# Copying the split state into an order by part before it goes to the output product's stack

## The chip, the core and the metric

The kernel runs on one core of a Trainium2 chip. Its engines are named as the profile names them: PE (matrix products; PEld is its weight load), DVE, ACT and POOL (elementwise work) and SP, which here only issues DMA transfers; ACT issues some transfers as well. An engine works through its own list of instructions in order and waits on semaphores for the others. The metric is the device time of one execution in microseconds (us). Before the change the median of three runs is 1157.68 us (1153.25 to 1157.78).

## The reference

A recurrence runs over 768 steps for 4 batches of 8 heads, each with a state of 40 x 40; its outputs, laid out as 3072 tokens of 320 numbers, pass through two gated layers.

```python
for t in range(S):
    kt, vt, rt = (k[:, :, t], v[:, :, t], r[:, :, t])
    wt, at, bt = (w[:, :, t], a[:, :, t], b[:, :, t])
    y[:, :, t] = np.einsum('bhd,bhde->bhe', rt, state)
    Sa = np.einsum('bhde,bhe->bhd', state, at)
    state_decay = state * wt[:, :, None, :] - np.einsum('bhd,bhe->bhde', Sa, bt)
    state = state_decay + np.einsum('bhd,bhe->bhde', vt, kt)

h = x @ w_in                     # 320 -> 2048
g = where(h >= 1, h, where(h <= -1, 0, (h + 1) ** 2 / 4))
x = g @ w_out                    # 2048 -> 320
g = x @ w_gate                   # 320 -> 1536
out = (g / (1 + exp(-g)) * (x @ w_val)) @ w_out2
```

## The kernel before, in words

The 768 steps are cut into 12 chunks of 64, and each chunk into four tasks, one for each batch (8 heads, 320 columns of state). Three streams of work share the engines.

- **Preparation** (`decay_tasks`, `p_tasks`, `inv_tasks`): products of the decays, the scaled inputs, the 64 x 64 matrices of a chunk, and on DVE the inverse of its triangular part, 31 steps of two small instructions (lines 915 and 920). The inverse is stored to `tsd` (line 938) and comes back for a task pair as `tt` (lines 1009 and 1013).
- **State** (`m_tasks`): a task multiplies the inputs with the state (line 1038), takes two rounds through the halves of the inverse (lines 1048 and 1054, with ACT and DVE splits at 1062, 1073 and 541 between them), forms the output product and the new state on PE (lines 1106 and 1127), and scales the state on DVE (1134, 1137).
- **Layers** (`in1`, `in2`, `outp`): 12 blocks of 256 tokens through both layers, PE lines 1170 and 1234, as each chunk's outputs come ready. Their weights arrive in pieces (line 607) that DVE (612 to 620), ACT and POOL bring into 16-bit form.

All numbers that PE multiplies are 16-bit pairs, a high and a low part. The new state is split so into the tile `ss`, partitions 64 to 103: for each head 120 columns, the parts high, low and high of 40 columns each (line 1140 on ACT, the helper `split`, line 541, on DVE). From `ss` it goes two ways. A transposing DMA (line 1148) makes `s0t[j]`, which the next chunk's line 1038 reads. And three DMAs (line 1152) put the three parts under each other into the stack `s0s[j]`, partitions 0 to 119, which the output product (line 1127) of the next chunk reads. Since a part of one head is 40 numbers wide, each of the three moves 40 partitions x 8 heads in runs of 80 bytes, 320 runs:

```python
for i in range(3):
    DMA(lambda e, i=i: e.dma_start(
        out=s0s[j][D * i:D * i + D], in_=G("ss", key)[q, :, D * i:D * i + D]),
        r=[("ss", n)], w=[("s0s", n)], use=SS, p=p + 8, dma=0.25, cost=0.84)
```

There are 44 tasks with such a state (none in the last chunk), so 132 of these DMAs and 42,240 runs.

The order of all instructions is planned when the kernel is built (class `Plan`). Each piece of work is recorded as a task with its engine, an assumed cost, what it reads and makes, the buffers it uses, and a due time `p`. The plan runs the tasks in a model of the engines, forwards and backwards in turn, and keeps the best order; a DMA goes to SP's list, or to ACT's where SP is busy in the model. A buffer of a pool (`ss` has one tile, and a second one for the first four tasks) is held from its first use to the end of its last, a DMA's landing included. Line 1265 holds the constants that set the due times: `LEAD` is how far ahead of its place in the period the state work of a chunk is due, `PLEAD` how far ahead of that the preparation, `BP` and `BM` shift chunk 0's, `DP` parts the halves of the decay work, `LSTEP` spaces the later weights. The tile `gf` is 128 partitions high, and only partitions 64 to 127 are written.

Of the kernel before, what the change touches and what calls it, by code (L numbers as in the profile page):

```python
# [8 lines left out]
F32 = mybir.dt.float32  # L9
F16 = mybir.dt.float16  # L10
# [312 lines left out]
def tile_recurrence__then__gated_mlps(  # L323
# [16 lines left out]
    B, H, S, D = r.shape  # L340
    BH = B * H
    HD = H * D
    C = 64
# [27 lines left out]
    v_, s_, p_, t_ = nc.vector, nc.scalar, nc.gpsimd, nc.tensor  # L371

    K = Plan()
    T, G = K.task, K.get

    def sbt(name, shape, dt, n=None):
        if n is None:
            return sb.tile(shape, dt, name=name)
        ts = [sb.tile(shape, dt, name=f"{name}{i}") for i in range(n)]
        K.pool(name, ts)  # L380
        return ts
# [25 lines left out]
    ss = sbt("ss", [128, H, 128], F16, 1)  # L407
    s0t = [sbt(f"s0t{i}", [128, H, 48], F16) for i in range(B)]
    s0s = [sbt(f"s0s{i}", [128, H, D], F16) for i in range(B)]
# [4 lines left out]
    sbt("vh", [128, H, D], F16, 1)  # L414
    sbt("xs", [128, H, D], F16, 2)
    sbt("tt", [128, 2, 2, H, HC], F16, 1)
    sbt("gf", [128, H, C], F32, 1)
    sbt("pf", [128, H, C], F32, 1)
    mx = sbt("mx", [128, 36 * NT], F16)
    K.pool("xt", [mx[:, 6 * NT * i:6 * NT * (i + 1)].rearrange("p (a t) -> p a t", a=6)  # L420
# [552 lines left out]
    def m_tasks(n, p):  # L973
        c, j = divmod(n, B)
# [4 lines left out]
        key, pk, mp = ("m", n), ("p", n), ("mp", n // 2)  # L979
        q = slice(64, 64 + D)  # L980
        VH, VS, PX, VT, WT, SS = (
            [(x, key)] for x in ("vh", "vss", "px", "vsT", "wt", "ss"))
# [7 lines left out]
        for o in (0, C):  # L990
            DMA(lambda e, o=o: e.dma_start(
                out=G("ldv", key)[o:o + C], in_=v[j, :, cs, :].rearrange("h t e -> t h e")),
                w=[(key, "v")], use=V, p=p - 4, dma=0.53)
        T("ACT", c_s(HD), lambda: s_.activation(
            out=G("ldv", key), in_=G("ldv", key), func=AF.Copy, scale=2.0**8), r=[(key, "v")],
          w=[(key, "vd")], use=V, p=p - 2)
        if j % 2 == 0:
            ps = slice(8 * j, 8 * j + 16)
            DMA(lambda e: e.dma_start(
                out=G("wa", mp).rearrange("p j h d -> p (j h) d"),  # L1000
                in_=was[c % 4, ps].rearrange("h t e -> t h e")),
                r=[("dec", c)], w=[(mp, "wa")], use=WA, p=p + 4, dma=1.06)
            if not last:
                DMA(lambda e: e.dma_start(
                    out=G("ff", mp)[q].rearrange("p j h d -> p (j h) d"),
                    in_=fdr[c][ps].unsqueeze(0).to_broadcast([D, 2 * H, D])),
                    r=[("f", c)], w=[(mp, "f")], use=FF, p=p + 4, dma=0.36, cost=0.68)
            td = tsd[c][:, :, :, ps]
            DMA(lambda e: e.dma_start(
                out=G("tt", mp)[0:64].rearrange("p f j h t -> p f (j h t)"),  # L1010
                in_=td.rearrange("f l s b t -> (l s) f (b t)")),
                r=[("tsd", c)], w=[(mp, "tt")], use=TT, p=p - 3, dma=0.5)
            DMA(lambda e: e.dma_start(
                out=G("tt", mp)[64:96].rearrange("p f j h t -> p f (j h t)"),
                in_=td[:, 0].rearrange("f s b t -> s f (b t)")),
                r=[("tsd", c)], w=[(mp, "tt")], use=TT, p=p - 3, dma=0.25, cost=0.68)

        T("ACT", c_s(HD), lambda: s_.activation(  # L1018
            out=G("vh", key), in_=G("ldv", key), func=AF.Copy),
          r=[(key, "vd")], w=[(key, "vh")], use=V + VH, p=p - 1)  # L1020
        e0, eng, cost = side(c in VLP, HD)
# [59 lines left out]
        for hf in range(2):  # L1081
# [3 lines left out]
              use=PX + XS[hf], p=p)  # L1085
# [45 lines left out]
        if not last:  # L1131
            y = lambda: hd(G(pg, (key, "y")))[q]
            if c:
                T("DVE", c_v(HD, True), lambda: v_.tensor_tensor(
                    out=y(), in0=y(), in1=sf[j][q], op=ALU.add),
                  r=[(key, "y"), ("sf", n - B)], w=[(key, "s1")], use=PY, p=p)
            T("DVE", c_v(HD), lambda: v_.tensor_tensor(
                out=y(), in0=y(), in1=G("ff", mp)[q, j % 2], op=ALU.mult),
              r=[(key, "s1") if c else (key, "y"), (mp, "f")], w=[(key, "s2")], use=PY + FF, p=p)
            T("ACT", c_s(2 * HD), lambda: s_.activation(  # L1140
                out=hi2(G("ss", key)[q]), in_=two(y()), func=AF.Copy, scale=2.0**-6),
              r=[(key, "s2")], w=[(key, "s3")], use=PY + SS, p=p)
            T("DVE", c_v(HD), lambda: split(
                G("ss", key)[q, :, D:2 * D], y(), 2.0**-6, G("ss", key)[q, :, 0:D]),
              r=[(key, "s3")], w=[("ss", n)], use=PY + SS, p=p)
            T("ACT", c_s(HD), lambda: s_.copy(out=sf[j][q], in_=y()), r=[(key, "s2")],
              w=[("sf", n)], use=PY, p=p)
            TR(lambda: nc.sync.dma_start_transpose(
                out=s0t[j], in_=flat(G("ss", key)[64:112])),
                r=[("ss", n)], w=[("s0t", n)], use=SS, p=p, dma=0.57)  # L1150
            for i in range(3):
                DMA(lambda e, i=i: e.dma_start(
                    out=s0s[j][D * i:D * i + D], in_=G("ss", key)[q, :, D * i:D * i + D]),
                    r=[("ss", n)], w=[("s0s", n)], use=SS, p=p + 8, dma=0.25, cost=0.84)
        xk = ("x", c, j // 2)
        xf = lambda: G("pf", (key, "x"))[vr].rearrange("p h t -> p (h t)")[:, 0:HD]
        XF = [("pf", (key, "x"))]
# [104 lines left out]
                    out=out[r0:r0 + C, :], in_=o()[64 * q:64 * q + 64]),  # L1262
                    r=[(ok, tt, 1)], w=[("out", c)], use=[("u", uk)], p=p, dma=0.31)

    PER, LEAD, PLEAD, DLEAD, WLEAD, ILEAD, WSTEP, LPRI, LSTEP, BP, BI, BM, DP, BD, P1, M1 = 69.67, 10.07, 94.28, 203.97, -34.92, 128.76, 0.3, 29.05, 2.22, -0.71, 2.76, 0.74, 10.0, 113.83, 18.78, 5.0
    SUP = PER / B

    def m0(n):
# [112 lines left out]
```

## Time and profile before

| | |
|---|---|
| median of 3 runs | 1157.68 us (1153.25 to 1157.78) |
| the profiled execution, its own time | 1155.31 us |
| its span on the core | 1153.6 us |
| PE busy in the span | 910.4 us (79%) |
| ACT, DVE, POOL busy | 866.0, 755.0, 569.0 us |
| DMA packets | 560948, of which 537140 under 512 bytes |

The profile is of one execution. Busy time leaves out the issuing of DMAs, which is listed as SPq or ACTq with the time that the instruction held that engine's list. An entry "A <- B" in a list of waits is idle time of A that ended when B was done; "issue" there is time in which the engine waited for nothing that the profile shows. PEclk is the granted TensorE clock, 1.00 for 2.4 GHz and 0.50 for 1.2 GHz.

### The profile page before, as it was taken

To read this page: it belongs to the slowest core of one execution; us is meant where nothing else is said; L and a number is where in the kernel's file an instruction comes from. 1 tells how busy PE (TensorE), PEld (TensorE's weight loads), DVE (VectorE), ACT (ScalarE), POOL (GpSimd) and SP (SyncE) were. 2 spreads that over 40 slices of the span, in tenths; PEclk is the share of its full clock that TensorE was granted. 3 is DMA by queue.
4 is the path that set the end of the run, shared out by engine and by line. 5 is a ranking of instruction groups with operands and counts; after the bars stand their busy time and mean duration, and the time that the engine had idled before them with its cause. 6 is when DMAs were issued, how large, how long until landed. Compare 5 with 4: busy or idle time off the path is not lost. (4 is left out here: it accounts for less than half of the span.)

```text
span 1153.6 us, 29900 instructions
## 1 busy us (share of the span) xinstructions
PE 910.4 (79%) x11328; PEld 745.1 (65%) x11328; DVE 755.0 (65%) x1830; ACT 866.0 (75%) x1628; POOL 569.0 (49%) x756
## 2 busy tenths in 40 slices
PE   0131246744789899989999899999999999999998
PEld 0131235533567777777777787787777777888886
DVE  7778796886879487585765856856758457442211
ACT  2595687876996998988979979788798796763422
POOL 5689634533566536545554545545545433322321
PEclk9999999766899999999999999999999999999999
DMA  9988699669979888787977877799667534321000
GB/s 212 240 200 169 182 149 159 147 116 197 195 145 152 122 124 143 134 129 126 147 121 126 134 123 128 127 134 140 103 130 129 101 75 76 60 44 32 4 15 23
DMA packets 560948, 144.63 MB, mean 125 GB/s; under 512 B 537140, under 2 KB 544820, under 8 KB 560804
## 3 DMA queue, kind: packets, MB, share of 16 engines
q1 hardware_dynamic: 523036, 135.08, 64.8%
q10 hardware_dynamic: 37768, 7.66, 4.3%
q8 instruction: 88, 1.44, 0.6%
q14 instruction: 56, 0.46, 0.2%
HBM read 74.87 MB, written 18.14 MB: 81 GB/s over the span
## 5 line engine op out<-in xcount | busy, mean ns | idle before, releaser
L539 POOL TENSOR_TENSOR mx<-mx 128x512 f16<-128x512 f32 x168 | 194.7, 1161 | 271.8 <-ACT mx L1190 252.1
L1234 PE MATMUL po<-wo,mx 128*128 128x320 f16 x2016 | 314.3, 302 | 3.9 <-DVE mx L541 2.5
L1234 PEld LDWEIGHTS <-mx 128*128 128x128 f16 x2016 | 191.1, 98 | 72.9 <-DVE mx L541 2.8
L1170 PE MATMUL ph<-mx,w 128*128 128x256 f16 x1536 | 194.0, 278 | 17.4 <-DMA mx<-x 10.1
L1170 PEld LDWEIGHTS <-w 128*128 128x128 f16 x1536 | 147.6, 99 | 41.7 <-issue 18.4
L1170 PE MATMUL ph<-x2t,wv 128*128 128x256 f16 x1152 | 141.3, 272 | 4.9 <-DVE mx L1220 3.2
L1170 PE MATMUL ph<-x2t,wg 128*128 128x256 f16 x1152 | 140.9, 273 | 2.3 <-ACT mx L1216 2.2
L1190 ACT CAST mx<-mx 128x512 f16<-128x512 f32 x168 | 102.9, 615 | 48.1 <-DVE mx L1220 30.1
L1206 DVE SCALAR_TENSOR_TENSOR mx<-ph,mx 128x512 f32<-128x512 f32 x96 | 66.2, 690 | 94.6 <-ACT mx L1203 94.2
L1170 PEld LDWEIGHTS <-wv 128*128 128x128 f16 x1152 | 110.4, 98 | 20.0 <-issue 6.5
L1170 PEld LDWEIGHTS <-wg 128*128 128x128 f16 x1152 | 109.8, 98 | 17.7 <-issue 2.9
L920 DVE TENSOR_TENSOR pg<-pg,ub 128x126 f32<-128x126 f32 (+22 forms) x372 | 96.4, 259 | 9.8
L915 DVE SCALAR_TENSOR_TENSOR ub<-ub,pg 128x126 f32<-128x126 f32 (+22 forms) x372 | 92.4, 248 | 14.5 <-DMA ub<-lsd 4.5
L1220 DVE SCALAR_TENSOR_TENSOR mx<-ph,mx 128x512 f32<-128x512 f32 x72 | 49.4, 686 | 71.9 <-PE ph L1170 69.0
L1062 ACT ACTIVATE xs<-px 32x320 f16<-32x320 f32 x176 | 75.0, 426 | 11.6 <-PE px L1054 6.1
L545 POOL TENSOR_TENSOR ldp<-ldp 128x320 f32<-128x320 f32 (+1 forms) x90 | 76.6, 864 | 11.8 <-ACT ldp L822 5.5
L1073 ACT ACTIVATE vss<-px 32x640 f16<-32x640 f32 x88 | 61.1, 695 | 12.3 <-PE px L1048 10.3
L1048 PEld LDWEIGHTS <-tt 96*32 96x32 f16 x768 | 28.5, 95 | 64.4 <-issue 45.2
L541 DVE SCALAR_TENSOR_TENSOR xs<-px,xs 32x320 f16<-32x320 f32 x88 | 42.6, 484 | 39.7 <-ACT xs L1062 37.3
L1202 ACT ACTIVATE mx<-ph 128x512 f32<-128x512 f32 x96 | 57.0, 594 | 12.6 <-PE ph L1170 10.5
L539 POOL TENSOR_TENSOR vss<-ldv,vh 128x320 f16<-128x320 f32 x48 | 38.5, 801 | 56.5 <-ACT vh L1018 25.0
L541 DVE SCALAR_TENSOR_TENSOR vss<-px,vss 32x320 f16<-32x320 f32 x88 | 43.4, 493 | 30.0 <-ACT vss L1073 24.8
(226 smaller groups left out, 1713.9 us busy)
## 6 DMA issues: line engine op xcount, KB each, us to landing
ldv<-in_v_dram SPq DMA_DIRECT2D x88, 80.0 KB
ub<-lsd SPq DMA_DIRECT2D x22, 256.0 KB
wo<-in_moe_w_out_dram SPq DMA_DIRECT2D x17, 320.0 KB
ldp<-was SPq DMA_DIRECT2D x23, 160.0 KB
out_dram<-mx SPq DMA_DIRECT2D x46, 80.0 KB
wo<-in_moe_w_in_dram SPq DMA_DIRECT2D x7, 512.0 KB
ldp<-in_b_dram SPq DMA_DIRECT2D x22, 160.0 KB
ldp<-wks SPq DMA_DIRECT2D x22, 160.0 KB
```

Source lines behind the costliest of these rows:

```text
L539: e.tensor_tensor(out=out, in0=x, in1=hi, op=ALU.subtract)
L541: e.scalar_tensor_tensor(out=out, in0=x, scalar=scale, in1=hi, op0=ALU.mult, op1=ALU.subtract)
L545: e.tensor_tensor(out=out, in0=x, in1=y, op=ALU.mult)
L915: v_.scalar_tensor_tensor(out=t, in0=L()[:, j, j + 1:].unsqueeze(1).to_broadcast([128, nm, ni]), scalar=-(2.0**-10), in1=m[:, 0:nm, j:j + ...
L920: v_.tensor_tensor(out=m[:, 0:nm, j + 1:], in0=m[:, 0:nm, j + 1:], in1=t, op=ALU.add)
L1062: s_.activation(out=xs[32 * i:32 * i + 32], in_=px[32 * hf:32 * hf + 32], func=AF.Copy, scale=-(2.0**-10))
L1073: s_.activation(out=hi2(G("vss", key)[z]), in_=two(hd(G("px", key))[z]), func=AF.Copy, scale=2.0**-8)
L1170: t_.matmul(out=ps, lhsT=wts[:, wi, fs], rhs=xT[:, xi, :], start=(i == 0), stop=(i == len(plan) - 1))
L1190: T("ACT", c_s(512), lambda: s_.copy(out=G("g", key)[:, 0], in_=u2(key)), r=[(key, "u")], w=[(key, "gh")], use=U + GG, p=p)
L1202: s_.activation(out=u2(key), in_=ps2(key), func=AF.Relu, scale=2.0**-8, bias=1.0)
L1206: T("DVE", c_v(512, True), lambda: v_.scalar_tensor_tensor(out=u2(key), in0=ps2(key), scalar=2.0**8, in1=u2(key), op0=ALU.max, op1=ALU.min ...
L1234: t_.matmul(out=ps, lhsT=g[:, x, f, 128 * tt:128 * tt + 128], rhs=wo[:, 2 * i + f, y, :], start=(i == 0 and f == 0 and m == 0), stop=(i == ...
```

## The change

The three parts are first copied, by one DVE instruction, into a new place `s2` of 40 partitions x 3 parts x 320 numbers, so that the eight heads of one part lie side by side. The three DMAs then read `s2` and write whole rows of the stack: each moves 40 runs of 640 bytes. `s2` is one buffer, in partitions 0 to 39 of `gf`, which were not used; the copy of a task cannot start before the three DMAs of the task before have landed. `ss` is now released when the copy and the transposing DMA are done. The plan's assumed costs for these DMAs go down, the copy is added with an assumed cost of 0.33 us, and six of the constants are changed.

```diff
-    sbt("gf", [128, H, C], F32, 1)
+    gf = sbt("gf", [128, H, C], F32, 1)[0]
+    K.pool("s2", [gf[0:D].rearrange("p h t -> p (h t)").bitcast(F16)[:, 0:3 * HD].rearrange(
+        "p (x y) -> p x y", x=3)])
...
+            S2 = [("s2", key)]
+            T("DVE", 0.06 + 3 * HD * 0.28e-3, lk=True, emit=lambda: v_.tensor_copy(
+                out=G("s2", key).rearrange("d x (h e) -> d x h e", h=H),
+                in_=G("ss", key)[q, :, 0:3 * D].rearrange("d h (x e) -> d x h e", x=3)),
+              r=[("ss", n)], w=[(key, "s2c")], use=SS + S2, p=p + 4)
             for i in range(3):
                 DMA(lambda e, i=i: e.dma_start(
-                    out=s0s[j][D * i:D * i + D], in_=G("ss", key)[q, :, D * i:D * i + D]),
-                    r=[("ss", n)], w=[("s0s", n)], use=SS, p=p + 8, dma=0.25, cost=0.84)
+                    out=s0s[j][D * i:D * i + D].rearrange("d h e -> d (h e)"), in_=G("s2", key)[:, i]),
+                    r=[(key, "s2c")], w=[("s0s", n)], use=S2, p=p + 8, dma=0.11, cost=0.68)
...
-    ... LEAD, PLEAD, ... LSTEP, BP, ... BM, DP ... = ... 10.07, 94.28, ... 2.22, -0.71, ... 0.74, 10.0 ...
+    ... LEAD, PLEAD, ... LSTEP, BP, ... BM, DP ... = ... 16.61, 96.27, ... 2.43, -5.96, ... 2.65, 6.56 ...
```

The new costs and constants move instructions on every engine, mostly by a few places. Of the 132 DMAs into the stack 98 are now issued by SP and 34 by ACT (87 and 45 before); over all transfers SP issues 945 and ACT 78 (932 and 91 before). Line numbers of the changed kernel are larger by 2 to 7.

The first place is SP's list where chunk 0's inverse is stored (`tsd_138`) and fetched again (`tt_115`); `wo_67`, `was` and `wks` are transfers of weights and of later decays. Before:

```order
L938 DMA tsd_138<-ub_121 32x32x32 x4
L607 DMA wo_67<-in_moe_w_out_dram 128x640
L864 DMA lsd_139<-gf_116 32x8x32
L729 DMA was_159<-wg 128x640
L729 DMA wks_160<-wg 128x640
L607 DMA wo_67<-in_moe_w_in_dram 128x2x512
L1009 DMA tt_115<-tsd_138 64x2x512
L1013 DMA tt_115<-tsd_138 32x2x512
```

Now, at the same place:

```order
L940 DMA tsd_138<-ub_121 32x32x32 x4
L866 DMA lsd_139<-gf_116 32x8x32
L609 DMA wo_67<-in_moe_w_out_dram 128x640
L1011 DMA tt_115<-tsd_138 64x2x512
L609 DMA wo_67<-in_moe_w_out_dram 128x640
L1015 DMA tt_115<-tsd_138 32x2x512
L866 DMA lsd_139<-gf_116 32x8x32 x2
L609 DMA wo_67<-in_moe_w_in_dram 128x2x512
```

The pair of decay stores now stands ahead of the `tsd` store, and the weight piece of 512 KB behind the fetch; a piece of 320 KB stands between its two halves.

The second place is DVE's list at the state of the first task of chunk 1: `ss_100` is the split state, lines 915 and 920 (917 and 922) are steps of a later chunk's inverse, `xs_114` the split that PE's line 1048 waits for. Before:

```order
L541 SCALAR_TENSOR_TENSOR xs_114<-px_124,xs_114 32x320
L915 SCALAR_TENSOR_TENSOR ub_121<-ub_121,pg_126 128x100
L612 TENSOR_SCALAR px_125<-wo_67 128x512
L920 TENSOR_TENSOR pg_126<-pg_126,ub_121 128x4x25
L541 SCALAR_TENSOR_TENSOR ss_100<-pg_127,ss_100 40x8x40
L915 SCALAR_TENSOR_TENSOR ub_121<-ub_121,pg_126 128x96
```

Now:

```order
L543 SCALAR_TENSOR_TENSOR ss_100<-pg_126,ss_100 40x8x40
L917 SCALAR_TENSOR_TENSOR ub_121<-ub_121,pg_127 128x81
L1154 COPY gf_116<-ss_100 40x960
L543 SCALAR_TENSOR_TENSOR xs_114<-px_124,xs_114 32x320
L922 TENSOR_TENSOR pg_127<-pg_127,ub_121 128x3x27
L614 TENSOR_SCALAR px_125<-wo_67 128x320
```

The state's split moved ahead of the next task's `xs`, and the copy (`gf_116` is the tile that holds `s2`) stands between the two, so that `xs` starts only after the copy.

## Rows read from the trace of the kernel before

**Rows 1.** Busy time by stretch: us, us (instructions) per engine, clock, DMA share, GB/s
```profile
core 0: us, PE busy (x) PEld busy (x) DVE busy (x) ACT busy (x) POOL busy (x), PEclk, DMA share, GB/s
0.00:180.00 180.00, 41.51 (x616) 35.67 (x617) 144.76 (x399) 114.07 (x197) 124.04 (x243) 1.00 0.88 189
180.00:320.00 140.00, 85.47 (x1081) 64.80 (x1081) 110.61 (x232) 110.15 (x210) 58.87 (x69) 0.78 0.83 163
320.00:1000.00 680.00, 633.91 (x8137) 521.27 (x8134) 462.67 (x1141) 575.18 (x1100) 344.04 (x404) 1.00 0.75 124
```
**Rows 2.** PE's waits over the run: us in total, times, longest
```profile
PE px L1048 <- DVE xs L541: 24.5, 27, 2.8
...
PE ph L1048 <- DMA tt<-tsd: 11.0, 2, 7.6
...
PE px L1054 <- DVE vss L541: 9.1, 13, 1.8
...
PE pg L853 <- DMA kbT<-lsp: 1.7, 2, 1.2
```
**Rows 3.** Timeline 108 to 126 us, queues and PE: start, duration, instruction
```profile
116.12 0.40 SPq L607 DMA_DIRECT2D wo<-in_moe_w_in_dram  x1
...
117.27 0.62 SPq L1013 DMA_DIRECT2D tt<-tsd  x1
...
121.87 0.42 PE L1048 MATMUL ph<-xs,tt 96*32 96x40 f16 x8 [7.64 <-DMA tt<-tsd]
```
**Rows 4.** The chain of work that ended last: start, duration of two transfers
```profile
707.64 2.10 DMA s0s<-ss
749.58 2.16 DMA tt<-tsd
```
**Rows 5.** Issues of the state's and of a 40-row transfer: duration ns min/median/max
```profile
L1152 SPq DMA_DIRECT2D s0s<-ss x83: 767/852/1429, 158.2 to 985.4; - x83
L1152 ACTq DMA_DIRECT2D s0s<-ss x43: 783/822/872, 154.9 to 982.6; - x43
...
L1004 SPq DMA_DIRECT2D ldp<-fdr x19: 301/463/1897, 57.2 to 945.5; - x19
L1004 ACTq DMA_DIRECT2D ldp<-fdr x3: 307/309/353, 152.2 to 528.2; - x3
```
**Rows 6.** Timeline 144 to 147 us, ACT's list and engine
```profile
144.75 1.42 ACTq L1152 DMA_DIRECT2D s0s<-mx  x1
...
146.22 0.47 ACT L956 ACTIVATE x<-pf 64x320 f16<-64x320 f32 x1 [0.94 <-issue]
```
**Rows 7.** Packets of the run and the main DMA queue, and the state's transfers
```profile
DMA packets 560948, 144.63 MB, mean 125 GB/s; under 512 B 537140, under 2 KB 544820, under 8 KB 560804
...
q1 hardware_dynamic: 523036, 135.08, 64.8%
...
s0s<-ss SPq DMA_DIRECT2D x83, 25.0 KB
```
**Rows 8.** DVE instructions by line: duration ns min/median/max, shapes
```profile
L723 DVE COPY wg<-wv x11: 172/175/179, 22.4 to 124.8; 32x40 f32<-32x40 f32 x11
...
L856 DVE TENSOR_TENSOR pg<-pg,mask x48: 677/699/700, 59.3 to 945.4; 128x512 f32<-128x512 f32 x48
...
L541 DVE SCALAR_TENSOR_TENSOR wg<-lsp,wg x2: 685/944/1202, 269.5 to 315.3; 64x512 f16<-64x512 f32 x2
```
**Rows 9.** DVE's waits over the run
```profile
DVE xs L541 <- ACT xs L1062: 37.3, 42, 3.6
DVE vss L541 <- ACT vss L1073: 26.6, 30, 2.4
```
**Rows 10.** Timeline 320 to 350 us, one state and its transfers
```profile
325.87 0.49 DVE L541 SCALAR_TENSOR_TENSOR ss<-pg,ss 40x320 f16<-40x320 f32 x1
...
339.38 0.83 SPq L1152 DMA_DIRECT2D s0s<-ss  x1
...
346.74 0.49 DVE L541 SCALAR_TENSOR_TENSOR ss<-pg,ss 40x320 f16<-40x320 f32 x1 [0.77 <-ACT ss L1140]
```

More of the change, by code (lines that the diff above doesn't have):

```diff
@@ L1263, in outp @@
                     r=[(ok, tt, 1)], w=[("out", c)], use=[("u", uk)], p=p, dma=0.31)
-    PER, LEAD, PLEAD, DLEAD, WLEAD, ILEAD, WSTEP, LPRI, LSTEP, BP, BI, BM, DP, BD, P1, M1 = 69.67, 10.07, 94.28, 203.97, -34.92, 128.76, 0.3, 29.05, 2.22, -0.71, 2.76, 0.74, 10.0, 113.83, 18.78, 5.0
+    PER, LEAD, PLEAD, DLEAD, WLEAD, ILEAD, WSTEP, LPRI, LSTEP, BP, BI, BM, DP, BD, P1, M1 = 69.67, 16.61, 96.27, 203.97, -34.92, 128.76, 0.3, 29.05, 2.43, -5.96, 2.76, 2.65, 6.56, 113.83, 18.78, 5.0
     SUP = PER / B
```

## The prediction

> **What bounds the kernel now.** I read the busy time by stretch first [rows 1]. From 320 to 1000 us PE is busy 633.9 of 680 us, so 46 us of that stretch are idle, and ACT is busy 575 us of it: PE is the bound there, with ACT close behind. Before 320 us it is otherwise: PE works 127 us of 320, while DMA is busy 0.83 to 0.88 and DVE and ACT each over 110 us of the 140 us from 180 to 320; the granted clock there averages 0.78, so part of PE's work ran at 1.2 GHz. The kernel's time is thus a start of some 320 us set by transfers and by the chain of state work, and then PE's own work with 46 us of gaps. After 1000 us the state work is nearly over and PE runs through the layers alone.
>
> Next come PE's waits over the run [rows 2]. The longest class that lies in the middle is the state's: `xs` 27 times and `vss` 13 times, 33.6 us in 40 waits, out of 144 such steps (48 tasks, line 1048 twice and line 1054 once in each). PE also waits for DMAs: six rows, of which the first (`tt`, 11.0 us) and the last (`kbT`, 1.7 us) are shown, 43.2 us in 17 waits. No row has PE waiting for `s0s`: the stack is read one period, some 70 us, after it is made. So neither the packets nor the copy stand on the path themselves; they count by what they take from DMA engines, queues, DVE and ACT.
>
> **The change, part by part.** Each term is in us of PE's path, in the profiled execution (1155.31 us: the span of 1153.6 and 1.7 around it), which is 2.4 under the median of 1157.68.
>
> *The start.* Chunk 0's state work begins when `tt` is there. Now its second fetch is issued at 117.27 and PE starts on it at 121.87, 4.6 us later, after an idle time of 7.64 [rows 3]; in a calm stretch such a fetch takes 2.16 [rows 4]. The weight piece of 512 KB that is issued at 116.12, right before, moves behind the fetch, and two decay stores move ahead of the inverse's store; a piece of 320 KB comes between the halves. I take the difference to the calm fetch, 4.6 - 2.2 = 2.4 us, as won. Bounds: nothing (the fetch waits for the store of the inverse, not for the piece), and 4.6.
>
> *SP's list.* An issue of these DMAs holds SP for 0.852 us, because each is cut into 320 runs. The nearest row to one with 40 whole rows is `ldp<-fdr`, 0.463 on SP and 0.309 on ACT [rows 5]. So 87 x 0.852 = 74 us become 98 x 0.463 = 45 us. What stands behind them on SP are transposes and fetches that PE waits for, 17 times. If half of these waits have one such issue just ahead, PE gains 8.5 x 0.389 = 3.3 us. Bounds: nothing (SP's list has slack), and all 17 with one, 6.6.
>
> *ACT's list.* 45 x 0.822 = 37 us become 34 x 0.309 = 11 us. Such an issue can cost ACT idle time: the one at 144.75 held the list for 1.42 and ACT then stood 0.94 with nothing to wait for [rows 6]. Were half of the saved 26 us idle time of ACT, and 40 of 144 steps of the state work seen by PE (0.28), the gain is 13 x 0.28 = 3.6; I take 3.0, since ACT often has an instruction in hand. Bounds 0 and 7.3 (all 26).
>
> *The DMA engines.* 42,240 runs become 5,280. By number of packets the old ones are 42,240 of 560,948, 7.5% of a busy time of some 0.69 x 1153.6 = 797 us per DMA engine (the main queue's 64.8% and 4.3% of the second), 60 us; by bytes 132 x 25.6 KB, 3.38 of 144.63 MB, 18.6 us [rows 7]. The new ones are 7.5 by number and 18.6 by bytes. The saving is between 0 and 52, and I take 26, 0.6 us for a task. It counts while transfers bound the kernel, for the 8 tasks of chunks 0 and 1: 4.7 us, of which I take 2.0. Bounds 0 and 4.7.
>
> *The copy.* 44 new DVE instructions of 40 x 960 numbers of 16 bits, 1920 bytes a partition. The trace has no such copy. From below: a copy of 40 numbers, 0.175. From above: at the pace of 512 numbers in 0.699 and 320 in about 0.49, about 1 ns a number, 1.16. The row nearest in bytes is the 128 x 512 in 32 bits, 2048 bytes, and I take its 0.70 [rows 8]. In all 31 us of DVE, which is busy 463 of 680 us in the middle stretch: most copies fall into idle time. Where one is followed at once by `xs`, as at the first state of chunk 1, PE may see it. Of 44 copies 0.28, so 12, should meet a step that PE waits for; but DVE itself waits for ACT before 72 of its 192 such splits [rows 9], and a copy goes into such a gap, so I count half of them, 6 x 0.70 = 4.2 us. Bounds 6 x 0.175 = 1.1 and 12 x 1.16 = 13.9.
>
> The Trainium skill (VectorE: DVE Perf Modes, The perf-mode tier table) has a copy of 16-bit numbers in SBUF at four numbers a cycle, against one for what rows 8 show; an estimate from that page is 0.16 + 0.25 = 0.41 us, and the term would be 2.5 instead of 4.2. No run here shows it yet. The Trainium skill also speaks against the copy (GPSIMD Engine Reference, Specifications): POOL shares its SBUF interfaces with DVE instructions that use two ports or two SBUF inputs. What rows 8 show agrees: the same 64 x 512 split takes 0.685 at best and 1.202 at worst. With POOL busy 344 of 680 us, an average loss of 0.13 us for each copy would add 0.8 to the term.
>
> *The new wait.* `s2` is one buffer, so the copy waits for the last task's three landings, with all of DVE behind it. Before, ACT's line 1140 waited in the same way for `ss`. I cost it at nothing because states are 8 to 40 us apart; the price when that cover goes is the second rival.
>
> *The order.* The other constants shift the preparation and the state by a few places; the state's split of the first task of chunk 1 now stands ahead of `xs`. I find no place that it clearly helps or hurts and give it 0, between -5 and +5: PE's gaps of 46 us in the middle depend on it.
>
> Sum: -2.4 - 3.3 - 3.0 - 2.0 + 4.2 = -6.5, so 1148.8 in the profiled execution. Against the median that is 2.4 more, 1151.2; I say 1151.0 us, 0.6% less.
>
> **Rivals.**
>
> *Hidden anyway.* PE does the same work from 320 us on, and a start shortened by 2.4 us is lost again where DVE, busy 145 us of the first 180 [rows 1], bounds the chunk: there the four copies alone take 2.8 us. The lists of SP and ACT have slack, and the copies cost 4.2 against the 2.0 from the DMA engines. That gives 1155.3 + 2.2 = 1157.5, and 1159.9 with the median's offset: within 0.5%. For it: no wait for `s0s` anywhere. Against it: the 43 us of waits for transfers, and 0.83 of DMA in the start.
>
> *The copy blocks DVE.* The three DMAs are due late (p + 8), and SP issues them late: after the split at 325.87 the last of them went at 339.38, and with its 0.83 and a landing of 2.10 was there at 342.3, where the next split starts at 346.74 [rows 4, 10]. That margin is 4.4 us, with 20.9 between the states. Where they are 8 to 12 us apart and SP as late, DVE stands for up to 6 us, and the splits for which PE waits stand behind the copy. One such wait of 4 us in each of 11 chunks is 44 us of DVE; a third of it on PE's path is 14.7, and with the copy's 4.2, nothing won on SP, and the other gains (-7.4), 1155.3 + 11.5 = 1166.8, with the offset 1169.2. It decides from the point where the last of the three DMAs lands later than the next split ends. For it: one buffer where ACT had more freedom, an in-order DVE. Against it: each issue is shorter now, and the same hold on `ss` cost little before. A bad draw of the order, +5 and more in the gaps, ends on this side too, at 1163 or above.
>
> *More than that.* The state's constants (LEAD from 10.07 to 16.61) make the plan bring the state work earlier, and PE's 33.6 us of waits for `xs` and `vss` shrink by a third, 11 us: 1140. Against it: the places on PE hardly differ. I count it with the forecast's side.
>
> **How the numbers follow.** A difference of 0.5%, 5.8 us, is about what a measurement of this kernel can tell from no change. The forecast has 0.36 (its own range 1144 to 1156, from the bounds of start, SP and copy), more than that 0.12, hidden anyway 0.32, the blocked DVE or a bad order 0.20. The forecast lies near the edge of 0.5%, 1151.9, so a little of it falls on no change; 0.46 for faster, 0.34 for the same, 0.20 for slower. The range reaches to the third rival's neighbourhood below and to the blocked DVE above: 1137 to 1167.
>
> **What would show it.** Right: issues of line 1152's successor at about 0.46 on SP and 0.31 on ACT; the DMA packets of the run down to some 524,000; PE's first wait for `tt` down from 7.64 to about 5; a copy of 0.4 to 0.7; PE's idle time from 320 to 1000 near 40 us. Wrong: DVE waiting for `s0s` in its list of waits by more than 10 us; PE's waits for `xs` grown; a start in which the first layer product does not come earlier; an issue as long as before, which would mean that the runs did not join.

## The result, and the profile after

The changed kernel takes 1170.47 us (median of 4 runs, 1169.53 to 1172.52) against 1157.38 us for the kernel before beside it: a ratio of 1.0126, with a 95% interval of 1.0109 to 1.0143. By that ratio it is some 14.6 us slower (the two medians lie 13.1 apart); 1151.0 with a range of 1137 to 1167 was forecast. The profiled execution took 1170.18 us, its span 1168.4.

The change did what it says: 36,958 packets are gone, where 42,240 - 5,280 is 36,960, and the transfers now come out of `gf`. Packets of the changed kernel and its main queue, to be read beside [rows 7]:

```profile
DMA packets 523990, 144.64 MB, mean 124 GB/s; under 512 B 494901, under 2 KB 507861, under 8 KB 523845
...
q1 hardware_dynamic: 499514, 136.38, 62.6%
```

Busy time by stretch, the view of [rows 1], here with 320 to 400 us as a row of its own:

```profile
core 0: us, PE busy (x) PEld busy (x) DVE busy (x) ACT busy (x) POOL busy (x), PEclk, DMA share, GB/s
0.00:180.00 180.00, 41.47 (x617) 35.20 (x618) 145.33 (x404) 115.50 (x198) 125.23 (x243) 0.66 0.86 192
180.00:320.00 140.00, 91.77 (x1162) 70.82 (x1162) 110.72 (x234) 111.56 (x213) 60.56 (x70) 0.76 0.78 158
320.00:400.00 80.00, 63.03 (x712) 49.93 (x711) 57.98 (x141) 61.61 (x117) 46.72 (x59) 0.91 0.86 143
320.00:1000.00 680.00, 617.89 (x7885) 504.03 (x7884) 482.91 (x1172) 563.30 (x1078) 338.87 (x399) 0.99 0.72 123
```

The row from 320 to 400 us of the kernel before, and the busy times of the whole changed kernel:

```profile
320.00:400.00 80.00, 72.55 (x832) 58.62 (x829) 55.97 (x138) 66.38 (x127) 51.58 (x64) 1.00 0.91 147
```
```profile
PE 915.4 (78%) x11328; PEld 745.4 (64%) x11328; DVE 779.8 (67%) x1874; ACT 865.8 (74%) x1628; POOL 570.1 (49%) x756
```

PE is idle for 62.1 us of the 680 where it was 46.1, so most of the loss is in PE's gaps after the start, with 20 us more of DVE in the same stretch. Not all of it is: PE is also busy for 915.4 us where it was 910.4, with 11328 matmuls in both, so of the 14.8 us by which the profiled span grew some 5 are busy time. The granted clock from 320 to 400 us is 0.91 where it was 1.00, so part of that work now ran at 1.2 GHz; how much of the 5 us this makes was not told apart. (The clock of 0.66 in the first stretch, 1.00 in [rows 1], is no difference in work: the clock's record in the kernel before begins only 185.6 us into the span, and PE takes 41.47 us for 617 instructions where it took 41.51 for 616.)

What is new on DVE, and the issues of the three transfers (duration in ns, min/median/max), which answer to [rows 8] and [rows 5]:

```profile
L1154 DVE COPY gf<-ss 40x960 f16<-40x960 f16 x40 | 25.9, 648 | 1.3
L1154 DVE COPY gf<-mx 40x960 f16<-40x960 f16 x4 | 2.6, 648 | 0.1
```
```profile
L1159 SPq DMA_DIRECT2D s0s<-gf x98: 706/788/1918, 143.2 to 995.1; - x98
...
L1159 ACTq DMA_DIRECT2D s0s<-gf x34: 719/768/1572, 143.9 to 994.0; - x34
```

The copy takes 0.648 us, 28.5 us for all 44, near the 0.70 taken. The last column of its row says more: DVE was idle for 1.3 us in all just ahead of the 40 copies, so nearly every copy began with DVE in the midst of other work. The issues fell only from 0.852 to 0.788 on SP and from 0.822 to 0.768 on ACT, not to 0.463 and 0.309.

PE's wait for the first `tt`, 7.64 in [rows 3], is now 6.7, the longest of the two in this row of its waits (us in total, times, longest):

```profile
PE ph L1050 <- DMA tt<-tsd: 8.2, 2, 6.7
```

The first layer product starts at 179.9 us instead of 180.9, so a gain of 1 us at the start is there. A timeline of the changed kernel shows what stands behind a copy, steps of the inverse on which the next chunk hangs:

```profile
347.49 0.27 DVE L917 SCALAR_TENSOR_TENSOR ub<-ub,pg 128x115 f32<-128x115 f32 x1
347.80 0.65 DVE L1154 COPY gf<-ss 40x960 f16<-40x960 f16 x1
348.48 0.28 DVE L922 TENSOR_TENSOR pg<-pg,ub 128x115 f32<-128x115 f32 x1
348.80 0.27 DVE L917 SCALAR_TENSOR_TENSOR ub<-ub,pg 128x110 f32<-128x110 f32 x1
```

### The profile page after: what moved, and what is told of

It is laid out like the page before. It is cut to its first block, busy times and chain, and to the rows that moved or that the text cites. A ratio compares the mean times of both kernels' runs of the same rounds, so it can differ in the third digit from the quotient of the medians.

```text
span 1168.4 us, 30004 instructions
## 1 busy us (share of the span) xinstructions
PE 915.4 (78%) x11328; PEld 745.4 (64%) x11328; DVE 779.8 (67%) x1874; ACT 865.8 (74%) x1628; POOL 570.1 (49%) x756
## 5 line engine op out<-in xcount | busy, mean ns | idle before, releaser
L1177 PE MATMUL ph<-mx,w 128*128 128x256 f16 x1536 | 193.8, 278 | 17.0 <-DMA mx<-x 11.2
L917 DVE SCALAR_TENSOR_TENSOR ub<-ub,pg 128x126 f32<-128x126 f32 (+22 forms) x372 | 92.5, 249 | 14.6 <-DMA ub<-lsd 4.8
L1209 ACT ACTIVATE mx<-ph 128x512 f32<-128x512 f32 x96 | 57.1, 595 | 14.2 <-PE ph L1177 10.7
L1223 ACT ACTIVATE mx<-ph 128x512 f32<-128x512 f32 x72 | 42.9, 596 | 32.9 <-PE ph L1177 32.1
L1210 ACT ACTIVATE mx<-mx 128x512 f32<-128x512 f32 x96 | 60.5, 630 | 3.1
```

The costliest lines, as they stand in the source:

```text
L917: v_.scalar_tensor_tensor(out=t, in0=L()[:, j, j + 1:].unsqueeze(1).to_broadcast([128, nm, ni]), scalar=-(2.0**-10), in1=m[:, 0:nm, j:j + ...
L1177: t_.matmul(out=ps, lhsT=wts[:, wi, fs], rhs=xT[:, xi, :], start=(i == 0), stop=(i == len(plan) - 1))
L1209: s_.activation(out=u2(key), in_=ps2(key), func=AF.Relu, scale=2.0**-8, bias=1.0)
L1210: s_.activation(out=u2(key), in_=u2(key), func=AF.Square, scale=2.0**3)
```

## The experiments

The change has three parts that can be had apart: the new transfers, the copy that they need, and the new order (constants and assumed costs). The theory was at first that the order carries the loss; the rivals were the copy's time on DVE and the copy's wait for the last landings. "Old order" means that all instructions stand exactly as in the kernel before, and the copy is emitted with the split, right behind it. The ratio is to runs of the kernel before on the same chip (medians 1154.57 to 1155.58), and a loss in us below is the ratio's part above 1 times that median.

| kernel | copy | order | us | ratio, 95% interval |
|---|---|---|---|---|
| c_old | whole | old constants, new plan | 1174.26 | 1.0162, 1.0147 to 1.0177 |
| c_new | none, old transfers | new constants, new plan | 1169.40 | 1.0112, 1.0091 to 1.0133 |
| m_in_old | whole | old | 1170.49 | 1.0128, 1.0115 to 1.0141 |
| runs80 | whole, straight | changed kernel's | 1170.38 | 1.0126, 1.0113 to 1.0139 |
| copy_short | 24 numbers a row | old | 1161.42 | 1.0047, 1.0031 to 1.0063 |
| copy_only | whole, not read | old | 1170.31 | 1.0135, 1.0115 to 1.0155 |
| copy_twice | two | old | 1196.94 | 1.0355, 1.0336 to 1.0375 |
| copy_pool | whole, on GpSimd | old | 1164.71 | 1.0079, 1.0063 to 1.0095 |
| short_in_new | 24 numbers a row | changed kernel's | 1161.87 | 1.0066, 1.0045 to 1.0087 |
| copy_late | whole, later place | old | 1184.21 | 1.0249, 1.0230 to 1.0268 |
| tiny_lstep | none, old transfers | LSTEP 2.25, new plan | 1163.24 | 1.0072, 1.0046 to 1.0098 |
| k_lead | none, old transfers | LEAD, PLEAD new, new plan | 1160.47 | 1.0045, 1.0028 to 1.0061 |
| no_copy | none | old | 1153.93 | 0.9992, 0.9981 to 1.0002 |
| none_in_new | none | changed kernel's | 1159.07 | 1.0032, 1.0018 to 1.0046 |
| draw_before_2 | none, old transfers | LSTEP 2.15, new plan | 1163.14 | 1.0072, 1.0056 to 1.0087 |
| draw_after_2 | whole | LSTEP 2.50, new plan | 1174.54 | 1.0171, 1.0155 to 1.0187 |

### Order or mechanism: c_old, c_new, m_in_old

The changed kernel with the old constants (c_old), and the kernel before with the new ones (c_new):

```diff
-    PER, LEAD, PLEAD, ... = 69.67, 16.61, 96.27, ... 2.43, -5.96, 2.76, 2.65, 6.56, ...
+    PER, LEAD, PLEAD, ... = 69.67, 10.07, 94.28, ... 2.22, -0.71, 2.76, 0.74, 10.0, ...
```

> The changed kernel with the constants of before (LEAD 10.07, PLEAD 94.28, LSTEP 2.22, BP -0.71, BM 0.74, DP 10.0), so that the copy and the packets are there and the plan is drawn with the old lead times. If the loss comes from the new constants: 1150 to 1160 us, and the MLP product number 800 stands again near 384 us instead of 390. If the copy (44 x 0.648 = 28.5 us of DVE) and its waits cost it: 1166 to 1173, with the same place near 390. If any new plan shifts the result at random by some 10 us: anything, and its loss lies in another stretch.

> The kernel before with the new constants alone: no copy, old packets. If the loss comes from the constants: 1165 to 1175 us, and the stretch from 308 to 390 us loses some 15 to 20 us of PE's layer work. If it comes from the copy: 1153 to 1160. If every new plan is a draw of its own: anything between 1145 and 1175.

The old order with the copy and the new transfers (m_in_old):

```diff
+            def slc():
+                split(G("ss", key)[q, :, D:2 * D], y(), 2.0**-6, G("ss", key)[q, :, 0:D])
+                v_.tensor_copy(out=s2..., in_=G("ss", key)[q, :, 0:3 * D]...)
-            T("DVE", c_v(HD), lambda: split(...),
+            T("DVE", c_v(HD), slc,
```

> The kernel before, with its own order of all instructions kept to the place; only the copy stands right behind the state's split on DVE and the three transfers read the copied state. If the loss comes from the order: 1151 to 1159 us, and by the terms of the prediction 1151 to 1153 if the lists of SP and ACT and the start had gained what was forecast, 1156 to 1159 if the issue of 0.79 instead of 0.46 leaves little to gain. If the copy and its wait cost the loss: 1165 to 1172.

All three lose, so the first theory falls as it stood: the mechanism alone costs 14.8 us in an unchanged order, and the constants alone cost 12.9 without any copy. The two do not add up, since the changed kernel has both and loses 14.6. Where the time goes differs too. This is the start of the n-th of the layers' matmuls (lines 1170 and 1234 of before) less its start in the kernel before, read from the starts in each trace, in us (one execution of each, so the last row lies up to 2.5 us from the ratios above):

| n | before at | m_in_old | copy_twice | no_copy | changed kernel | none_in_new | c_new |
|---|---|---|---|---|---|---|---|
| 400 | 322.8 | 5.8 | 8.7 | -0.9 | -14.6 | -17.6 | -17.1 |
| 800 | 384.1 | 6.7 | 12.9 | -0.9 | 5.8 | 1.1 | 8.4 |
| 2000 | 580.2 | 12.7 | 23.6 | -1.0 | 11.4 | 2.8 | 11.9 |
| 3000 | 738.3 | 15.6 | 30.6 | -1.6 | 13.9 | 4.9 | 15.9 |
| last | 1149.2 | 17.2 | 41.3 | -3.4 | 14.9 | 2.0 | 15.8 |

In the old order the copy's loss grows steadily, as it would where each of 44 copies costs a little. In the new orders the layers are 15 to 18 us ahead at first and lose that and more between 320 and 390 us, where the fourth chunk's state is not there earlier (its first line 1048 at 387.1 us, before at 387.7) and PE runs out of work.

### The copy's time, its wait, the transfers

Fewer numbers (copy_short), 80-byte transfers out of `ss` with a copy that nobody reads (copy_only), the copy made twice (copy_twice), and on GpSimd (copy_pool), each against m_in_old:

```diff
-   out=s2..., in_=...
+   out=s2...[:, :, :, 0:1], in_=...[:, :, :, 0:1]
```

> The old order with the mechanism in it, but the copy takes 24 numbers of each row instead of 960 (the rest of the copied state is a constant, so the state's second product is left out of the result). Every wait stands, the copy still waits for the last landings and the transfers for it; only its 0.65 us shrink to some 0.1. If the copy's time on DVE is the loss: 1154 to 1159 us, since 44 x 0.5 us leave DVE. If the wait of the copy for the landings is the loss: 1168 to 1172, as with the whole copy. If the new transfers are: 1168 to 1172 as well.

```diff
-   out=s0s[j][D * i:D * i + D].rearrange("d h e -> d (h e)"), in_=s2[:, i]
+   out=s0s[j][D * i:D * i + D], in_=G("ss", key)[q, :, D * i:D * i + D]
```

> The old order and the old transfers, 320 runs each out of the split state; the copy is made right behind the split and nobody reads it, so that it waits for nothing. If the copy's time on DVE is the loss: 1168 to 1172 us. If the wait for the landings or the new transfers are: 1154 to 1158.

```diff
+   v_.tensor_copy(out=s2..., in_=...)
```

> The old order with the mechanism in it and the copy made twice, one right behind the other: 28.5 us more of DVE and no new wait. If the copy's time on DVE is the loss, some 0.3 us of each 0.65 reach PE's path: 1180 to 1187 us, or more if DVE becomes the bound in places. If the wait or the transfers are the loss: 1170 to 1174.

```diff
-   v_.tensor_copy(out=s2..., in_=...)
+   p_.tensor_copy(out=s2..., in_=...)
```

> The old order with the mechanism in it and the copy on GpSimd, at the same place of the program. If only the time on DVE is the loss: 1154 to 1160 us, since GpSimd has idle time and the copied state is read one period later. If an in-order engine that stands before the split and the landings is what costs, GpSimd's splits of the layers stand behind it and PE waits for them: 1162 to 1175, with waits of line 1241's products for GpSimd well above the 1 us of before.

A copy that nobody reads and that waits for nothing costs as much as the whole mechanism (ratios of 1.0135 and 1.0128): neither the wait for the landings nor the new transfers are the cause. The dose is: the short copy takes 0.254 us, 11.2 us in all, and costs 5.4; the whole one 28.5 for 14.8; two 57.0 for 41.0. That is 0.49, 0.52 and 0.72 us of the kernel for each us of DVE, and 0.92 for the second copy alone. These three are net of the 0.9 us that the new transfers win (no_copy, below); copy_only, which has the old transfers, gives the copy alone as 15.6 us. (1161.4 and 1196.9 both lie above what the theory had expected.) The copy rows of copy_short, copy_only and copy_pool:

```profile
L1148 DVE COPY gf<-ss 40x24 f16<-40x24 f16 x42 | 10.7, 254 | 1.4
```
```profile
L1147 DVE COPY gf<-ss 40x960 f16<-40x960 f16 x42 | 27.2, 648 | 1.4
```
```profile
L1147 POOL COPY gf<-ss x42: 979/979/980, 155.7 to 991.6; 40x960 f16<-40x960 f16 x42
...
  DVE ss L543: 39.0, 23
```

The last line is what GpSimd waited for ahead of its copies: 39.0 us in 23 waits for the split. DVE is rid of the copy, but now GpSimd, in its turn in order, stands before it. 1164.7 us is what the second theory expected; its sign, PE's waits for GpSimd at line 1241, rose to 2.3 us only, so which wait carries these 9 us is open. The starts of the layers' matmuls tell where they are lost: number 400 is 6.1 us late and the last one 8.9, against 5.8 and 17.2 in m_in_old. So after 322.8 us, where PE is the bound, the copy on GpSimd loses 2.8 us and the copy on DVE 11.4; the loss before that is the same on either engine, and its cause is open.

PE's waits for DVE from 320 to 1000 us, the five largest rows, show the dose as well. Engine and line, what it waited for, us, times, longest; first the kernel before, then m_in_old, then copy_twice:

```profile
PE px L1048 <- DVE xs L541: 15.7, 20, 1.5
PE px L1054 <- DVE vss L541: 5.5, 10, 1.6
PE ph L1170 <- DVE mx L1206: 4.7, 5, 2.2
PE pg L1127 <- DVE wt L539: 4.6, 11, 1.1
PE ph L1170 <- DVE mx L1220: 3.2, 5, 1.7
```
```profile
PE px L1050 <- DVE xs L543: 18.6, 19, 1.9
PE ph L1177 <- DVE mx L1213: 7.2, 8, 3.2
PE ph L1177 <- DVE mx L1227: 6.5, 7, 2.4
PE px L1056 <- DVE vss L543: 5.8, 11, 1.6
PE pg L1129 <- DVE wt L541: 5.0, 13, 1.1
```
```profile
PE px L1050 <- DVE xs L543: 23.6, 22, 2.6
PE px L1056 <- DVE vss L543: 11.5, 16, 2.6
PE ph L1180 <- DVE mx L1216: 11.0, 9, 3.9
PE ph L1180 <- DVE mx L1230: 8.2, 6, 3.1
PE pg L1129 <- DVE wt L541: 5.2, 13, 1.1
```

33.7, 43.1 and 59.5 us. The waits grow in number (51, 58, 66) and in length, and more than half of the first step (5.8 of 9.4) lies in the layers' combination, which the prediction did not count at all.

### The place of the copy: copy_late

```diff
+            if k in ("u", "h"):
+                free()
...
+            if k == "d" and held:
+                sent.append((t["emit"], eng))
+                continue
```

Here `u` is DVE's combination of a layer's products, `h` the next state's split, `d` a transfer, and `free` emits the held copy and then its transfers.

> The old order with the mechanism in it; the copy no longer stands right behind the split but is put ahead of the next instruction of DVE that combines a layer's products (39 of 44 so; 5 stand ahead of the next state's split), where DVE waits for ACT or PE anyway; the three transfers go behind it. If it is the place that costs (a copy ahead of the inverse's steps and of the next xs): 1156 to 1161 us. If it is the mere 28.5 us of DVE: 1167 to 1172.

Both were wrong: 28.8 us slower, as much as the copies take in all. DVE "waits" 94.2 us for ACT ahead of line 1206 in the kernel before, and still 87.5 here. The rows of DVE's waits for copy_late, and PE's waits from 320 to 1000 us:

```profile
DVE mx L1239 <- ACT mx L1235: 87.5, 57, 5.1
DVE mx L1254 <- PE ph L1202: 67.1, 21, 4.8
```
```profile
PE ph L1202 <- DVE mx L1254: 9.8, 11, 3.0
PE ph L1202 <- DVE mx L1239: 7.8, 9, 2.7
```

PE now waits 17.6 us for the combination (7.9 before, 13.7 in m_in_old). Of the loss, 10.7 us are there at the layers' matmul 500 (at 340.5 us in the kernel before), ahead of which all 5 forced places lie (151.7 to 269.6 us); from there to number 4500 it is 15.4 against 12.7 in m_in_old. Why the start suffers so much was not taken apart further.

### What the transfers win: no_copy, runs80

No copy, whole rows out of a constant tile (no_copy); and in the changed kernel a straight copy, out of which the transfers pick 80-byte runs (runs80):

```diff
-   v_.tensor_copy(out=s2..., in_=...)
+   v_.memset(gf[0:D], 0.0)
```

> The old order without any copy; the three transfers move whole rows out of a constant tile (the state's second product is left out of the result), so that only the new transfers are left of the change, and they wait for nothing. If they win what the prediction gave them (start 2.4, SP 3.3, ACT 3.0, DMA engines 2.0): 1143 to 1148 us. If an issue of 0.79 instead of 0.85 and hidden transfers leave nothing: 1153 to 1157.

```diff
-   out=G("s2", key).rearrange("d x (h e) -> d x h e", h=H), in_=....rearrange("d h (x e) -> d x h e", x=3)
+   out=G("s2", key), in_=G("ss", key)[q, :, 0:3 * D]
-   out=s0s[j][D * i:D * i + D].rearrange("d h e -> d (h e)"), in_=G("s2", key)[:, i]
+   out=s0s[j][D * i:D * i + D], in_=G("s2", key)[:, :, D * i:D * i + D]
```

> The changed kernel with a straight copy: the copied state keeps the order of the split, and the three transfers pick 320 runs of 80 bytes out of it, as in the kernel before. Order, copy and waits stay as in the changed kernel, apart from the copy's own pattern. If the larger packets are worth what was forecast for the DMA engines (2.0, at most 4.7) and for the start: 1172 to 1176 us. If they are hidden: 1169 to 1172. The issue stays at 0.77 to 0.79 on SP if its length does not hang on the runs, and is 0.85 if it does.

With no copy the new transfers are worth 0.9 us (0.0008 of the time; the interval is 2.2 faster to 0.2 slower). The profile has PE idle for 43.8 us from 320 to 1000 where it was 46.1:

```profile
320.00:1000.00 680.00, 636.21 (x8139) 522.33 (x8135) 463.43 (x1143) 577.75 (x1103) 344.36 (x405) 1.00 0.71 124
```

In runs80 all 36,959 packets are back and the ratio is 1.0126 again. Its straight copy takes 0.511 us on average (0.406 at the median, see the last section), so 6 us of DVE are saved beside, which at the 0.4 to 0.5 above would be some 2 to 3 us. The shorter packets can have cost about that much, give or take the 2.5 us to which the two ratios are known. The copy's row and its issues, by line:

```profile
L1154 DVE COPY gf<-ss 40x960 f16<-40x960 f16 x40 | 20.4, 511 | 1.3
```
```profile
L1158 SPq DMA_DIRECT2D s0s<-gf x98: 767/844/1678, 143.6 to 994.5; - x98
...
L1158 ACTq DMA_DIRECT2D s0s<-gf x34: 783/830/1409, 143.3 to 993.9; - x34
```

So 320 runs in place of 40 cost 0.06 us of an issue, and the rest of 0.79 has another cause.

### The changed kernel's own loss: none_in_new, short_in_new

In the changed kernel's order, the copy's emission is left out (none_in_new), or takes 24 numbers a row (short_in_new):

```diff
-   emit=lambda: v_.tensor_copy(out=G("s2", key)..., in_=G("ss", key)...)
+   emit=lambda: None
```

> The changed kernel's own order without any copy, transfers out of a constant tile as above. What stands above the kernel before is then the order's share of the loss. From the short copy in the same order (1161.9 with 44 x 0.254 = 11.2 us of DVE): if each us of DVE costs 0.5, 1155 to 1158 and the order costs next to nothing; if the short copy was hidden in the planner's room, 1160 to 1163 and the order costs 5 to 7.

> The changed kernel with its own order, but the copy takes 24 numbers of each row instead of 960 (0.254 instead of 0.648 us; the rest of the copied state is a constant, so the state's second product is left out of the result). It parts the changed kernel's loss into copy and order. If the planner gave the copy room: 1168 to 1171 us, no gain, and the whole loss is the order's. If the copy costs here what it cost in the old order (0.53 us for each us of DVE): 17.3 x 0.53 = 9 us less, 1160 to 1163, and the order takes some 4 us of the loss.

Without the copy this order takes 3.7 us more than the kernel before, between the two expectations; with the short one 7.6, with the whole one 14.6. So the copy is worth 10.9 us here, 0.38 us for each us of DVE (0.35 for the short one), somewhat less than in the old order; the planner did find it room, but not enough. With the 0.9 that the transfers win, the order costs 4.6. PE's idle time from 320 to 1000 us goes along: 53.0 us in none_in_new (the row below), 56.8 in short_in_new, 62.1 in the changed kernel.

```profile
320.00:1000.00 680.00, 627.05 (x8012) 511.63 (x8010) 462.93 (x1141) 567.39 (x1089) 337.89 (x397) 0.99 0.71 123
```

### Is it these constants, or any: k_lead, tiny_lstep, draw_before_2, draw_after_2

```diff
-    ... LEAD, PLEAD, ... LSTEP, ... = ... 10.07, 94.28, ... 2.22, ...
+    ... LEAD, PLEAD, ... LSTEP, ... = ... 16.61, 96.27, ... 2.22, ...
```

This is k_lead, in the kernel before; tiny_lstep and draw_before_2 have 2.25 and 2.15 for its 2.22 alone, and draw_after_2 has 2.50 for the changed kernel's 2.43.

> The kernel before with only LEAD 16.61 and PLEAD 96.27 (the state work and its preparation due 6.5 and 8.5 us earlier). If these two carry the 13.9 us that all six new constants cost: 1166 to 1173 us. If LSTEP or DP carry them: 1153 to 1160. If every new draw costs: 1162 to 1172, and the stretch where it is lost differs from that of the other draws.

> The kernel before with one constant moved by a hair: LSTEP 2.25 instead of 2.22 (the late weight pieces are due 0.03 us further apart each), which alters the planner's order in thousands of places. If every new draw of the order costs, since the order of before is the best of many: 1162 to 1172 us, with no meaning in the constant. If it takes the large shifts of LEAD and LSTEP to do harm: 1153 to 1159.

> The kernel before with LSTEP 2.15 instead of 2.22, a second draw of the order by a constant that means little. If the order of before is the best of many: 1158 to 1170 us. If the first such draw (7.7 us slower) was bad luck: 1150 to 1157.

> The changed kernel with LSTEP 2.50 instead of 2.43, a second draw of its order with the copy. If the copy costs some 8 us in any order and draws scatter by 5 to 14 us on top: 1165 to 1178. If the changed kernel's own draw is a bad one: 1158 to 1166.

A constant moved by 0.03 us, or by 0.07 the other way, costs 8.3 us each time, and k_lead's two constants 5.2, less than either theory had them cost if they mattered. The five new plans without a copy, c_new and none_in_new among them, are 3.7 to 12.9 us slower than the order of before, with no pattern in the constant; with the copy, three plans are 14.6, 18.7 and 19.7 slower. So the order of before is a good draw, and a new plan for whatever reason gives part of that up. That these five all lose does not show that none could win.

## Why the prediction was wrong

Term by term, for the changed kernel: the start, the two lists and the DMA engines won 0.9 us instead of 10.7 (no_copy, in the old order), the copy cost 10.9 instead of 4.2, and the order 4.6 instead of 0. The misses of 9.8, 6.7 and 4.6 make up the 21.1 us between the forecast of -6.5 and the 14.6 measured; each is known to some 2 us. Had any one of the three come as forecast, the change would still have lost.

- **The first step that failed is the copy's overlap.** Its price for one was right (0.70 taken, 0.648 measured), its share on the path was not: "a copy goes into such a gap, so I count half of them, 6 x 0.70 = 4.2 us". It cost 15.6 us in the old order (copy_only), above the upper bound of 13.9, and 10.9 in its own, so 0.35 or 0.25 us for each of 44, not 0.1. The four largest rows of DVE's waits are 94.2 and 69.0 us (lines 1206 and 1220) and the two of [rows 9], 227.1 together, in the kernel before. In m_in_old they are still 218.5:

```profile
DVE mx L1213 <- ACT mx L1210: 87.5, 65, 4.6
DVE mx L1227 <- PE ph L1177: 68.3, 21, 4.4
DVE xs L543 <- ACT xs L1064: 32.2, 34, 3.5
DVE vss L543 <- ACT vss L1075: 30.5, 33, 2.4
```

  Only some 9 of the 28.5 us fell into them. I read that as follows: such a wait is no slack, because what DVE waits for was itself released by DVE's last result. When DVE is 0.65 us later, ACT and PE are, and the wait comes back in full behind the copy. The dose from 11 to 57 us agrees; the ring itself was not cut.
- **The second is the gain of SP's and ACT's lists, the start and the DMA engines**, 10.7 us together: measured 0.9. The prediction took the 320 runs for the reason of the 0.852 us, and the issue without them from the nearest row, a fetch from DRAM with 40 rows (0.463 and 0.309); it is 0.788 and 0.768, and runs80 puts the 320 runs at 0.06. By the prediction's own sums that leaves 0.5 and 1.5 of the two terms of 3.3 and 3.0. The prediction said that an issue as long as before would mean that the runs had not joined; they had, and it was nearly as long. The start gained 1 of the forecast 2.4 at the first layer product (1.9 to 2.5 in runs80, short_in_new and none_in_new, which have the same order), and nothing of it is left at the end. The packets went as forecast and were worth nothing that the runs can tell from zero.
- **The order**, 0 between -5 and +5: 4.6, inside the bounds. But these were too narrow for what a new plan does here, 3.7 to 12.9 in five plans without the copy, and the five all lie on one side of the 0 that I took.
- **The rivals.** "The copy blocks DVE" gave 1169.2, close to 1170.5, for a reason that is wrong: it had DVE stand for the landings, and copy_only, which waits for none, is as slow; in the changed kernel no wait of DVE for these transfers is listed. Its second half, a bad draw, is a third of the loss. "Hidden anyway" was right on the transfers and took the copy at 4.2. "More than that" had PE's waits for `xs` and `vss` shrink by a third through earlier state work: the state did not come earlier (387.1 against 387.7 us for the fourth chunk), and the two rows went from 33.6 to 32.0 us.

Of the prediction's four signs of being wrong none came as it was put: DVE lists no wait for `s0s`, PE's waits for `xs` went from 24.5 to 22.8 us, the first layer product came earlier, and the issue was a little shorter. What rose instead are PE's waits for DVE as a whole, from 152.3 to 163.2 us over all listed rows, and those for ACT, from 17.9 to 26.3, each spread over many rows. In m_in_old, where only the mechanism is new, the waits for `xs` did grow, to 28.8.

No version with the copy beat the kernel before, and in the old order no_copy shows what the transfers alone win: 0.9 us.

## What to carry to other kernels

Where two engines pass work to each other in turn, do not take idle time of the less busy one for room. In this kernel an instruction put there cost a third to the whole of its time; price it so until a trial with a shorter or a doubled one says otherwise. Doubling a suspected cost, and making it useless but keeping it, each in an order frozen to the place, parts cost, wait and benefit in three runs. And where a planner orders the program, a constant moved by nothing in particular shows what any new plan costs; a change that is worth less than that scatter has to be tried in the old order.

## What the runs showed of the hardware

- A DVE copy of 40 x 960 16-bit numbers takes 0.648 us when it reorders runs of 40 numbers, and 0.254 for 24 numbers; on GpSimd the reordering one takes 0.979. When both sides lie straight (runs80), the median is 0.406, in ns:

```profile
L1154 DVE COPY gf<-ss x40: 405/406/1249, 214.5 to 992.2; 40x960 f16<-40x960 f16 x40
```

  The prediction's estimate of 0.41 from the Trainium skill (VectorE: DVE Perf Modes, The perf-mode tier table) agrees with this copy, and not with the one that reorders, for which it was made. At two numbers a cycle instead of four the same sum would be 0.16 + 0.50 = 0.66, an estimate from that page, which is near the 0.648.
- A GpSimd instruction beside it did not change the copy that reorders: 25 of the 44 in m_in_old had one beside them, all 44 took 647 to 649 ns, and GpSimd's busy time is 569.13 us against 569.02 before. The straight copy was longer only beside one: in runs80 the 23 with none beside them took 405 to 407 ns, and of the 21 with one 12 took 459 to 1249, as here:

```profile
520.41 1.16 POOL L541 TENSOR_TENSOR mx<-mx 128x512 f16<-128x512 f32 x1
520.61 1.22 DVE L1154 COPY gf<-ss 40x960 f16<-40x960 f16 x1
```

  The Trainium skill (GPSIMD Engine Reference, Specifications) warns of this sharing of SBUF interfaces for DVE instructions that use two ports or two SBUF inputs. The straight copies of runs80 agree; that the copy that reorders does not use two ports would fit its even times, but no run shows it.
- An issue of an SBUF to SBUF transfer of 25.6 KB took 0.79 us on SP with 40 runs and 0.84 with 320 (the changed kernel and runs80). Why a 40-row fetch from DRAM issues in 0.463 was not tried.
